# Two halves of one PSUM tile become two tiles in the first MLP, and double tiles in the second

## The chip, the core and the metric

The kernel runs on one core of one Trainium2 chip. The metric is the device time of one execution in microseconds. Before the change it is 1389.45 us, the median of three runs (1388.26 to 1395.5).

## The reference

Three stages run one after the other. Attention reads float32 inputs, the weights are float64, and the result is float32, 4608 rows and 512 columns:

```python
# attention in chunks of 64 tokens, 8 batches, 8 heads, 576 tokens, head size 64
scores = scale * np.matmul(q_c, k_c.transpose(0, 1, 2, 4, 3))
scores = scores - np.max(scores, axis=-1, keepdims=True)
attn = np.exp(scores)
attn = attn / (np.sum(attn, axis=-1, keepdims=True) + 1e-09)
out = np.matmul(attn, v_c)
# first MLP, 512 -> 2048 -> 512
h = x @ w_in
g = np.maximum(h, 0.0) + np.log1p(np.exp(-np.abs(h)))
x = g @ w_out
# second MLP, 512 -> 768 -> 512
h = np.maximum(np.maximum(x @ w1, x @ w2), x @ w3)
return (h @ w_out).astype(np.float32)
```

## The kernel before

**Splitting and blocks.** The kernel keeps about float32 precision by cutting each operand into a high and a low part and running three matmuls for each product: high with high, high with low, low with high (`PASS`, line 26). Tokens go in 9 blocks of 512 (`TB`). A matmul writes 128 rows by 512 float32 columns, which is one PSUM bank.

**Order of the work.** No engine decides at run time. Every piece of work is an `Op` with an engine, an estimated cost, a due time and the buffers (`Buf`) that it reads, writes or takes. `Plan.order` (line 106) runs a small list scheduler over them: it starts the ready operation that is due first on each engine, gives it a free place of the kind that its `Buf` names (`places`, line 214), and returns all operations in order of their planned start. They are then issued in that order (line 1599). The framework below looks at the tiles that each instruction touches and adds the semaphore waits. So the order on each engine is fixed, and an instruction that must wait holds up everything behind it on its engine. Operations of TensorE's long products are chained in one line (`in_line("h", ...)`), so that they keep the order of the program.

**First MLP, blocks 0 to 2.** `mlp1` (line 782) computes for each of 16 columns blocks `j` of the hidden layer 12 matmuls into `ph` (line 791), a softplus on ACT from `ph` into a `tmp` (line 801), the cut of that into `g`, and 12 matmuls into the accumulators `acc` (line 811). Meanwhile the float64 weights are turned into float32 parts on DVE (`conv`, `cut_up`; a sum of two parts goes through `ph` by two small matmuls, lines 398 and 399), and the attention of later tiles goes through `aps`.

**First MLP, blocks 3 to 8.** Pairs of blocks are computed with seven products instead of eight (`UnitA`, line 1067; Strassen's method). Each unit has one `ph` (`u.Y`), into which products 1, 6, 7 and 4 go one after the other, copied out in between, and uses a shared pair of banks `XZ` (tile `one`): product 2 goes to half `X`, products 5 and 3 to half `Z`, and DVE adds each to what was kept (lines 1084, 1100, 1104, 1110). Two units overlap, an old and a new one. The attention that is left runs in the same two halves (`square_of`, line 580; lines 535 to 555), and `mlp1_out` (line 1150) does the second product of the MLP into `acc` (line 1190).

**Second MLP.** `Triple` (line 1255) takes three blocks at a time and computes their hidden layers with 15 products of sums instead of 18, each 12 matmuls into a pair of banks (line 1328), which are read as one wide operand by ACT or DVE. Four pairs are used in turn (`Bank`, line 1228): `ph`, `one` and the two `acc`. The last product (line 1426) accumulates into the same four pairs.

**The tiles of the change.** `ph` is one tile of two banks, `pairh` (line 213), and the two places of the kind `ph` are its halves (line 242). In the second MLP the same tile is used whole: `halves = [Buf("ph") ...]` (line 1530). `aps` is a tile of its own pool (line 204); when the Strassen products begin, `one_by_one` (line 1207) closes that pool and puts one tile of two banks, `one`, in its place, of which `X` and `Z` are the halves:

```python
pairh = psum.tile([P, 2, TB], F32, name="ph")
"ph": [pairh[:, n] for n in range(2)],
one_of.append(single.tile([P, 2, TB], F32, name="one"))
return [one_of[0][:, n] for n in range(2)]
```

Of the kernel before, what the change touches and what calls it, by code (L numbers as in the profile page):

```python
# [10 lines left out]
F32 = mybir.dt.float32  # L11
# [6 lines left out]
PSUM = bass.MemoryType.PSUM  # L18
DRAM = bass.MemoryType.DRAM

P = 128
# [162 lines left out]
def tile_kernel(ctx: ExitStack, tc: tile.TileContext, q, k, v, w_in, w_out, w1, w2, w3, wo2, out):  # L184
# [10 lines left out]
    TB = 512  # L195
# [4 lines left out]

    pool = ctx.enter_context(tc.tile_pool(name="sb", bufs=1))
    psum = ctx.enter_context(tc.tile_pool(name="ps", bufs=1, space=PSUM))
    banks = ExitStack()
    pair_of_banks = banks.enter_context(tc.tile_pool(name="pa", bufs=1, space=PSUM))
    dram = ctx.enter_context(tc.tile_pool(name="dr", bufs=1, space=DRAM))

    def mem(kind, n, shape, dt, where=pool):
        return [where.tile(shape, dt, name=f"{kind}{i}") for i in range(n)]
# [1 line left out]
    ident = pool.tile([P, P], F32, name="ident")  # L210
    small = {"mx": mem("mx", 4, [P, H], F32), "rq": mem("rq", 1, [P, TB], F32)}

    pairh = psum.tile([P, 2, TB], F32, name="ph")
    places = {

        "w": list(range(32)),
# [22 lines left out]
        "rv": mem("rv", 1, [P, TB], F32),  # L239
        "p": mem("p", 1, [P, TB], F32),  # L240
        "pd": [dram.tile([P, TB], F32, name=f"pd{i}") for i in range(2)],
        "ph": [pairh[:, n] for n in range(2)],
        "aps": mem("aps", 1, [P, 2, TB], F32, pair_of_banks),
        "acc": mem("acc", 2, [P, 2, TB], F32, psum),
        **small,
# [693 lines left out]
    def pe2(cost, fn, **kw):  # L939
        o = in_line("h", op({"P": cost}, fn, due=clock[0], **kw))  # L940
        clock[0] += cost
        return o
# [124 lines left out]
    class UnitA:  # L1067
# [8 lines left out]
        def product(u, p, dst, first, **kw):  # L1076
            at, col, name = SEVEN[p]
            ws, x = u.ws[at], x2["a", u.q, name]
            col += HT * (u.n % 2) if at == 3 else 0

            def fn(e):
                for kk in range(2):
                    for wi, xi in PASS:
                        nc.tensor.matmul(  # L1084
                            dst(),
                            ws.t[:, wi, col + kk * P:col + (kk + 1) * P],
                            x[kk].t[:, xi],
                            start=(first and kk == 0 and wi == 0 and xi == 0),
                            stop=(kk == 1 and wi == 1),
                            skip_group_check=not first,  # L1090
                        )

            return pe2(1.36, fn, r=[ws, *x], hold=u.ring[at] + held["a", u.q, name], **kw)
# [108 lines left out]

    second = {}

    one_of = []

    def one_by_one(_):

        banks.close()
        single = ctx.enter_context(tc.tile_pool(name="pb", bufs=1, space=PSUM))  # L1210
        one_of.append(single.tile([P, 2, TB], F32, name="one"))
        return [one_of[0][:, n] for n in range(2)]

    XZ = Buf("aps", fresh=one_by_one)

# [39 lines left out]
    class Triple:  # L1255
# [44 lines left out]
                lambda: wide(XL.t), lambda: wide(R[z].t), lambda: wide(XH.t).bitcast(F32), ALU.subtract, [R[z], XH], [XL], n=1.77  # L1300
            )

        def product(u, s, d):
            if s not in u.x:
                u.split(s)
            XH, XL, token = u.x[s]
            if u.q == 0 and d in DIRECT:
                ws, ring = direct[s, d]
            else:
                ws, ring = slot("w", "x"), Buf("ringb")  # L1310
                o = op(
                    {"G": 1.0},
                    lambda e: nc.gpsimd.dma_start(out=ws.t.bitcast(F32), in_=w2c[s][d]),  # L1313
                    w=[ws],
                    alloc=[ring, ws],
                    after=[store["c", s, d]],
                    lat=2.0,
                    move=2.2,
                )
                in_line("ringb", o)  # L1320
            bank = u.spare if s in (0, 12) else u.main[d]
            first = s in (0, 1, 12)

            def fn(e):
                for f in range(2):
                    for kk in range(2):
                        for wi, xi in PASS:
                            nc.tensor.matmul(  # L1328
                                bank.view()[:, f],
                                ws.t[:, wi, f * HT + kk * P:f * HT + (kk + 1) * P],  # L1330
                                (XH, XL)[xi].t[:, kk],
                                start=(first and kk == 0 and wi == 0 and xi == 0),
                                stop=(kk == 1 and wi == 1),
                                skip_group_check=not first,
                            )

            o = pe2(2.72, fn, r=[ws, XH, XL], w=bank.bufs, alloc=bank.new(), hold=[ring, token])
            u.read(s, d, bank)
            return o

# [119 lines left out]
    def strassen():  # L1460

        outs, earlies = [], 0
        tile_at = HP * NP + 2 * HP + 2

        def out(n=1):
            for out_of, *which in outs[:n]:
                out_of(*which)
            del outs[:n]

        def group():  # L1470
            nonlocal tile_at
            if tile_at <= NTILE + 1:
                attention(tile_at, [first_loads[11]], True)
            tile_at += 1

        splita(0)
        pairs = (NB - NP) // 2
        for q in range(pairs):
            A, B = NP + 2 * q, NP + 2 * q + 1
            old = None  # L1480
            for n, m in enumerate(ORDER[q]):
                clock[0] = T0 + STEP * NJ * A + 17.7 * n
                new = UnitA(q, m)
                begin = new.p1()
                for _ in range(EARLIES[q][n]):
                    early(earlies, clock[0] + STEP * EARLY, [begin])
                    earlies += 1
                if q == pairs - 1:
                    mark[n] = begin
                out()  # L1490
                if old:
                    old.p5()
                    old.p4()
                    outs.append((mlp1_out, A, 2 * old.n + 1))
                new.p6()
                if old:
                    old.p3()
                else:
                    out()
                new.p2()  # L1500
                if not old:
                    out()
                new.p7()
                if n in GROUPS:
                    group()
                out()
                outs.append((mlp1_out, A, 2 * m))
                old = new
            clock[0] = T0 + STEP * NJ * A + 17.7 * (NJ // 2)
            mark["load", q] = begin  # L1510
            mark["late", q] = old.p4()
            outs.append((mlp1_out, A, 2 * m + 1))
            out()
            old.p5()
            out()
            old.p3()
            todo = [(mlp1_out, B, 2 * m + f) for m in ORDER[q] for f in range(2)]
            outs.extend((*todo[i], (h,)) for h in range(2) for i in range(2))
            outs.extend(todo[2:])
            for j in range(NJ - 2):  # L1520
                out()
                if j in LATE_GROUPS:
                    group()
                if j == SPLIT and q + 1 < pairs:
                    splita(q + 1)
        mark[5] = mark[6]
        clock[0] = T1
        for d, at in enumerate((mark["late", 1], mark[4], mark["late", 2])):
            weights3(d, [at])
        halves = [Buf("ph") for _ in range(2)]  # L1530
        accs = [Buf("acc") for _ in range(2)]
        banks = [Bank(halves, lambda: pairh), Bank([XZ], lambda: one_of[0])]
        banks += [Bank([z], lambda z=z: z.t) for z in accs]
        D = range(NJ2 // 2)
        gate = [mark[5]]
        for q in range(NB // 3):
            u = Triple(q, banks, gate)
            u.g = {}
            todo = [(s, d) for d in D for s in (0, 1)] + [(s, d) for s in range(2, 12) for d in D]
            todo += [(s, d) for d in D for s in (12, 13)] + [(14, d) for d in D]  # L1540
            if q == 0:
                todo[:6] = [(0, 0), None, None, (1, 0), None, None, (0, 1), (0, 2), (2, 0), (1, 1), (1, 2)]
                todo = [p for n, p in enumerate(todo) if p != (2, 0) or n < 11]
            for p in todo:
                if p is None:
                    out()
                    continue
                begin = u.product(*p)
                if p == (13, 0):
                    gate = [begin]  # L1550
            for c in range(3):
                for d in D if (q, c) != (NB // 3 - 1, 2) else D[:-1]:
                    u.out(c, d)
            banks = [u.main[1], u.main[2], u.spare, u.main[0]]
        for h in range(2):
            u.out(2, D[-1], range(2 * h, 2 * h + 2))
# [5 lines left out]
    for n, f in enumerate((1.0, -1.0)):  # L1562
# [3 lines left out]
            w=[(eye, n)],  # L1566
# [66 lines left out]
```

## Time and profile before

| | before |
|---|---|
| median of 3 runs (lowest to highest) | 1389.45 us (1388.26 to 1395.5) |
| profiled execution, its own time | 1391.89 us |
| its span, first to last instruction | 1390.1 us |
| mean granted TensorE clock | 0.992 |
| PE (matmuls) busy | 1349.2 us, 97% |
| PEld (weight loads) busy | 1104.5 us, 79% |
| DVE busy | 940.0 us, 68% |
| ACT busy | 486.8 us, 35% |
| POOL busy | 303.1 us, 22% |

PE is TensorE's matmuls, PEld its weight loads, DVE VectorE, ACT ScalarE, POOL GpSimd, SP the engine that issues most DMAs. The profile names an instruction by the line of the kernel that made it (L791), often a helper's: L276 and L278 are copies, L283 is every two-operand operation of DVE. In the timeline a row is one instruction or several of the same kind that follow each other; its first number is when it began, the second how long it took, and in brackets stands how long its engine had stood idle before it and what ended that. `ph` and `one` name a whole tile there, without the half.

### The profile page before, as it was taken

The page shows a single profiled execution, that of the slowest core. Times are in us where ns is not written, and L with a number is a line of the kernel's source. Part 1 is how long each engine was busy: PE and PEld are TensorE (multiplying, and loading weights), DVE is VectorE, ACT ScalarE, POOL GpSimd, SP SyncE. Part 2 cuts the span into 40 slices and gives each one's busy share as a digit, 9 for nine tenths or more (in the row PEclk, how much of TensorE's full clock was granted, in tenths as well). Part 3 has the DMA queues.
Part 4 walks back from the last instruction along what each step waited for, and adds up shares of the span by engine and source line. Part 5 has one row for each costly group of instructions (what it writes and reads, how often), then busy time and mean ns, then how long its engine had stood idle before and what let it go on. Part 6 is the DMA issues. An engine that isn't in the chain of part 4 may idle for free.

```text
span 1390.1 us, 22779 instructions
## 1 busy us (share of the span) xinstructions
PE 1349.2 (97%) x8664; PEld 1104.5 (79%) x8664; DVE 940.0 (68%) x1510; ACT 486.8 (35%) x790; POOL 303.1 (22%) x532
## 2 busy tenths in 40 slices
PE   5899999999999999999999999999999999999998
PEld 3677877788788788887888878788888888888887
DVE  8899976698576846637856686459824497244951
ACT  4444323354433524344434453433113221132211
POOL 2001545542142303312122112112101111011100
PEclk9999999999999999999999999999999999999999
DMA  9545657675688977857979899556644466444401
GB/s 275 163 142 141 155 162 216 189 256 175 201 238 277 258 201 210 276 172 273 314 261 341 277 359 371 197 182 227 226 168 137 151 218 221 152 152 136 151 15 76
DMA packets 221772, 288.84 MB, mean 208 GB/s; under 512 B 122096, under 2 KB 147120, under 8 KB 221664
## 3 DMA queue, kind: packets, MB, share of 16 engines
q0 software_dynamic: 49728, 163.53, 34.7%
q1 hardware_dynamic: 171120, 123.08, 29.2%
q8 instruction: 68, 1.11, 0.3%
q10 hardware_dynamic: 816, 0.79, 0.2%
q14 instruction: 40, 0.33, 0.1%
HBM read 200.28 MB, written 87.03 MB: 207 GB/s over the span
## 4 chain that ended last, share of the span: by engine, by line
PE 82%; DVE 9%; DMA 4%; issue 2%; SPq 1%; ACT 1%; POOL 1%; DVEq 0%; ACTq 0%; POOLq 0%
PE acc L1190 17%; PE acc L1328 14%; PE ph L1084 8%; PE one L1328 8%; PE one L1084 6%; PE ph L791 5%; PE acc L811 5%; PE ph L1328 5%; PE acc L1426 5%; PE one L1426 3%; PE ph L1426 3%; DVE s L283 1%; DVE tmp L283 1%; PE one L583 1%; DVE tmp L346 1%
## 5 line engine op out<-in xcount | busy, mean ns | idle before, releaser
L1190 PE MATMUL acc<-g,s 128*128 128x512 f32 x1152 | 278.0, 394 | 3.8 <-DVE g L283 2.2
L1190 PEld LDWEIGHTS acc<-g,s 128*128 128x128 f32 x1152 | 216.2, 189 | 52.3 <-DVE g L283 4.7
L283 DVE TENSOR_TENSOR s<-s,s 128x512 fp32r<-128x512 f32 (+3 forms) x252 | 222.8, 906 | 41.6 <-ACT s L276 33.0
L276 ACT CAST s<-s 128x1024 fp32r<-128x1024 f32 (+1 forms) x140 | 115.3, 839 | 244.8 <-DVE s L283 86.9
L1328 PE MATMUL acc<-s,s 128*128 128x512 f32 x852 | 200.1, 389 | 0.0
L1328 PEld LDWEIGHTS acc<-s,s 128*128 128x128 f32 x852 | 159.9, 188 | 33.2
L283 DVE TENSOR_TENSOR g<-tmp,g 128x512 fp32r<-128x512 f32 x132 | 90.1, 684 | 94.3 <-ACT g L276 92.1
L791 PE MATMUL ph<-s,s 128*128 128x512 f32 x576 | 143.5, 400 | 4.7 <-ACT tmp L801 4.7
L1313 POOL DMA_DIRECT2D s<-w2c x120 | 63.9, 533 | 365.8 <-PE acc L1328 105.5
L1084 PE MATMUL ph<-s,s 128*128 128x512 f32 x576 | 142.9, 389 | 0.0
L811 PE MATMUL acc<-g,s 128*128 128x512 f32 x576 | 139.8, 392 | 0.1
L791 PEld LDWEIGHTS ph<-s,s 128*128 128x128 f32 x576 | 109.6, 192 | 30.2 <-ACT tmp L801 6.5
L1084 PEld LDWEIGHTS ph<-s,s 128*128 128x128 f32 x576 | 108.2, 188 | 22.6
L811 PEld LDWEIGHTS acc<-g,s 128*128 128x128 f32 x576 | 107.3, 188 | 23.3 <-ACT tmp L276 0.5
L1328 PE MATMUL one<-s,s 128*128 128x512 f32 x468 | 112.4, 389 | 0.0
L1084 PE MATMUL one<-s,s 128*128 128x512 f32 x432 | 106.2, 389 | 0.0
L1328 PEld LDWEIGHTS one<-s,s 128*128 128x128 f32 x468 | 87.8, 188 | 18.2
L276 ACT CAST g<-tmp 128x512 fp32r<-128x512 f32 x128 | 79.4, 621 | 48.5 <-PE acc L1190 34.4
L1084 PEld LDWEIGHTS one<-s,s 128*128 128x128 f32 x432 | 81.1, 188 | 16.8
L463 POOL DMA_DIRECT2D rv<-in_v_dram x102 | 62.0, 612 | 142.2 <-PE one L583 95.3
L1110 ACT ACTIVATE tmp<-tmp 128x512 f32<-128x512 f32 x72 | 45.0, 632 | 126.9 <-DVE tmp L283 126.8
L283 DVE TENSOR_TENSOR tmp<-one,tmp 128x512 f32<-128x512 f32 x72 | 48.1, 685 | 52.1 <-PE one L1084 48.6
(138 smaller groups left out, 1648.2 us busy)
## 6 DMA issues: line engine op xcount, KB each, us to landing
s<-w2c POOLq DMA_DIRECT2D x120, 512.0 KB, 4.3
s<-wac POOLq DMA_DIRECT2D x66, 512.0 KB, 5.9
w2c<-s POOLq DMA_DIRECT2D x45, 512.0 KB, 5.5
wac<-s POOLq DMA_DIRECT2D x24, 512.0 KB, 5.2
gd<-tmp SPq DMA_DIRECT2D x48, 256.0 KB, 4.4
x2d<-tmp SPq DMA_DIRECT2D x36, 256.0 KB, 4.3
s<-in_moe_w_dram POOLq DMA_DIRECT2D x18, 512.0 KB, 5.1
tmp<-gd SPq DMA_DIRECT2D x36, 256.0 KB, 5.0
```

The lines of the kernel that those rows point to most:

```text
L276: nc.scalar.copy(dst(), src())
L283: return op({"D": 0.69 * n}, lambda e: nc.vector.tensor_tensor(dst(), a(), b(), f), r=r, w=w, **kw)
L346: lambda e: nc.vector.scalar_tensor_tensor(ai(), hw(), -0x40000000, ai(), ALU.bitwise_and, ALU.bitwise_or),
L463: dma(out=dst().rearrange("p (c e d) -> p c e d", e=2, d=D)[half * CH:(half + 1) * CH, lo:lo + mine, h, :], in_=v[b, t % HP * 2 + h].rearr ...
L791: nc.tensor.matmul(ph.t, w[:, wi, kk * P:(kk + 1) * P], x[kk].t[:, xi], start=(kk == 0 and wi == 0 and xi == 0), stop=(kk == KD - 1 and wi ...
L811: nc.tensor.matmul(acc[m // 2].t[:, m % 2], w[:, wi, m * P:(m + 1) * P], g.t[:, gi, :], start=(first and wi == 0 and gi == 0), stop=(last ...
L1084: nc.tensor.matmul(dst(), ws.t[:, wi, col + kk * P:col + (kk + 1) * P], x[kk].t[:, xi], start=(first and kk == 0 and wi == 0 and xi == 0), ...
L1110: in_line("y", op({"A": 0.62}, lambda e: nc.scalar.activation(c.t, src(), AF.Softplus), r=[z], w=[c], alloc=[] if z is c else [c]))
L1190: nc.tensor.matmul(acc[half].t[:, m % 2], w.t[:, wi, m * P:(m + 1) * P], g.t[:, gi, :], start=(first and wi == 0 and gi == 0), stop=(last ...
L1313: lambda e: nc.gpsimd.dma_start(out=ws.t.bitcast(F32), in_=w2c[s][d]),
L1328: nc.tensor.matmul(bank.view()[:, f], ws.t[:, wi, f * HT + kk * P:f * HT + (kk + 1) * P], (XH, XL)[xi].t[:, kk], start=(first and kk == 0 ...
L1426: nc.tensor.matmul(banks[t // 2].view()[:, t % 2], (GH, GL)[gi].t[:, f, t * P:(t + 1) * P], wo2_of[j].t[:, wi], start=(j == 0 and wi == 0 ...
```

## The change

The change makes the two halves of `ph` two tiles of one bank, in a pool of their own, and the two halves `X` and `Z` of `one` two tiles as well. When the second MLP begins, `four_banks` closes both pools and puts two tiles of two banks, `both`, in their place. For that the first product of the second MLP takes three places together: the two of `ph` and the one of `aps`. The second MLP's first two pairs of banks are then these double tiles. The accumulators, all loops and all costs and due times stay.

```diff
--- before.py
+++ after.py
@@ -200,6 +200,8 @@
 
     pool = ctx.enter_context(tc.tile_pool(name="sb", bufs=1))
     psum = ctx.enter_context(tc.tile_pool(name="ps", bufs=1, space=PSUM))
+    halves = ExitStack()
+    pair_of_halves = halves.enter_context(tc.tile_pool(name="pp", bufs=1, space=PSUM))
     banks = ExitStack()
     pair_of_banks = banks.enter_context(tc.tile_pool(name="pa", bufs=1, space=PSUM))
     dram = ctx.enter_context(tc.tile_pool(name="dr", bufs=1, space=DRAM))
@@ -210,7 +212,6 @@
     ident = pool.tile([P, P], F32, name="ident")
     small = {"mx": mem("mx", 4, [P, H], F32), "rq": mem("rq", 1, [P, TB], F32)}
 
-    pairh = psum.tile([P, 2, TB], F32, name="ph")
     places = {
 
         "w": list(range(32)),
@@ -239,7 +240,7 @@
         "rv": mem("rv", 1, [P, TB], F32),
         "p": mem("p", 1, [P, TB], F32),
         "pd": [dram.tile([P, TB], F32, name=f"pd{i}") for i in range(2)],
-        "ph": [pairh[:, n] for n in range(2)],
+        "ph": mem("ph", 2, [P, TB], F32, pair_of_halves),
         "aps": mem("aps", 1, [P, 2, TB], F32, pair_of_banks),
         "acc": mem("acc", 2, [P, 2, TB], F32, psum),
         **small,
@@ -1202,14 +1203,16 @@
 
     second = {}
 
-    one_of = []
-
     def one_by_one(_):
-
         banks.close()
-        single = ctx.enter_context(tc.tile_pool(name="pb", bufs=1, space=PSUM))
-        one_of.append(single.tile([P, 2, TB], F32, name="one"))
-        return [one_of[0][:, n] for n in range(2)]
+        single = banks.enter_context(tc.tile_pool(name="pb", bufs=1, space=PSUM))
+        return mem("one", 2, [P, TB], F32, single)
+
+    def four_banks(_):
+        banks.close()
+        halves.close()
+        again = ctx.enter_context(tc.tile_pool(name="pq", bufs=1, space=PSUM))
+        return mem("both", 2, [P, 2, TB], F32, again)
 
     XZ = Buf("aps", fresh=one_by_one)
 
@@ -1300,7 +1303,7 @@
                 lambda: wide(XL.t), lambda: wide(R[z].t), lambda: wide(XH.t).bitcast(F32), ALU.subtract, [R[z], XH], [XL], n=1.77
             )
 
-        def product(u, s, d):
+        def product(u, s, d, alloc=()):
             if s not in u.x:
                 u.split(s)
             XH, XL, token = u.x[s]
@@ -1334,7 +1337,7 @@
                                 skip_group_check=not first,
                             )
 
-            o = pe2(2.72, fn, r=[ws, XH, XL], w=bank.bufs, alloc=bank.new(), hold=[ring, token])
+            o = pe2(2.72, fn, r=[ws, XH, XL], w=bank.bufs, alloc=[*alloc, *bank.new()] if not alloc else alloc, hold=[ring, token])
             u.read(s, d, bank)
             return o
 
@@ -1527,9 +1530,9 @@
         clock[0] = T1
         for d, at in enumerate((mark["late", 1], mark[4], mark["late", 2])):
             weights3(d, [at])
-        halves = [Buf("ph") for _ in range(2)]
+        both = [Buf("ph"), Buf("ph"), Buf("aps", fresh=four_banks)]
         accs = [Buf("acc") for _ in range(2)]
-        banks = [Bank(halves, lambda: pairh), Bank([XZ], lambda: one_of[0])]
+        banks = [Bank(both[:1], lambda: both[2].t[0]), Bank(both[1:], lambda: both[2].t[1])]
         banks += [Bank([z], lambda z=z: z.t) for z in accs]
         D = range(NJ2 // 2)
         gate = [mark[5]]
@@ -1545,7 +1548,7 @@
                 if p is None:
                     out()
                     continue
-                begin = u.product(*p)
+                begin = u.product(*p, alloc=both if both[0].first is None else [])
                 if p == (13, 0):
                     gate = [begin]
             for c in range(3):
```

## Rows read from the trace of the kernel before

**Rows 1.** The page: the span, and part 1, busy us (share) xinstructions.

```profile
span 1390.1 us, 22779 instructions
...
PE 1349.2 (97%) x8664; PEld 1104.5 (79%) x8664; DVE 940.0 (68%) x1510; ACT 486.8 (35%) x790; POOL 303.1 (22%) x532
```

**Rows 2.** The list of waits: engine line <- released by: us, times, longest us.

```profile
PE ph L791 <- ACT tmp L801: 4.7, 5, 2.2
...
PE ph L398 <- ACT tmp L801: 2.8, 1, 2.8
PE one L583 <- DMA s<-gd: 2.7, 1, 2.7
...
PE acc L1190 <- DVE g L283: 2.2, 4, 0.8
...
ACT tmp L1110 <- PE ph L1084: 27.8, 21, 1.4
```

**Rows 3.** Timeline, 79 to 87: start us, us, engine, line, operation, xcount, [idle before <-releaser].

```profile
79.87 5.60 PE L791 MATMUL ph<-s,s 128*128 128x512 f32 x24
...
85.51 0.60 ACT L801 ACTIVATE tmp<-ph 128x512 f32<-128x512 f32 x1 [2.71 <-PE ph L791]
...
86.16 3.01 PE L791 MATMUL ph<-s,s 128*128 128x512 f32 x12 [0.69 <-ACT tmp L801]
```

**Rows 4.** Timeline, 344 to 347: `ph`, then `one`, then the copy of `ph`.

```profile
344.12 1.52 PE L1084 MATMUL ph<-s,s 128*128 128x512 f32 x6
...
345.48 1.52 PE L1084 MATMUL one<-s,s 128*128 128x512 f32 x6
345.68 0.59 ACT L276 COPY tmp<-ph 128x512 f32<-128x512 f32 x1 [3.49 <-PE ph L1084]
```

**Rows 5.** Timeline, 254 to 263, around the longest wait of L791.

```profile
254.90 0.58 ACT L801 ACTIVATE tmp<-ph 128x512 f32<-128x512 f32 x1
...
255.53 7.36 PE L791 MATMUL ph<-s,s 128*128 128x512 f32 x24 [2.18 <-ACT tmp L801]
```

**Rows 6.** Stretches: length; PE, PEld, DVE, ACT, POOL busy (count); granted clock; DMA share, GB/s.

```profile
113.00:180.00 67.00, 66.89 (x410) 54.30 (x409) 67.00 (x139) 25.71 (x44) 21.93 (x35) 1.00 0.52 133
257.00:259.00 2.00, 2.00 (x7) 1.51 (x6) 2.00 (x4) 0.00 (x0) 0.89 (x3) 0.50 0.29 71
644.00:646.00 2.00, 2.00 (x6) 1.52 (x6) 2.00 (x5) 0.33 (x2) 0.64 (x1) 0.50 1.03 405
```

**Rows 7.** Timeline, 36 to 63, the start of the first MLP.

```profile
36.56 0.63 PE L399 MATMUL ph<-s,s 128*128 128x512 f32 x1
...
41.88 0.69 DVE L283 TENSOR_TENSOR s<-ph,tmp 128x512 fp32r<-128x512 f32 x1 [3.52 <-PE ph L791]
...
49.80 0.69 PE L498 MATMUL aps<-ident,s 64*64 64x64 f32 x32 [1.31 <-DMA s<-in_v_dram]
...
50.32 0.65 PE L498 MATMUL acc<-s,s 64*64 64x64 f32 x32
...
51.71 0.68 DVE L558 TENSOR_REDUCE mx<-acc 128x8 f32<-128x512 f32 x1
...
61.83 0.69 PE L498 MATMUL acc<-ident,tmp 64*64 64x64 f32 x32 [1.22 <-ACT s L276]
```

**Rows 8.** Timeline, 458 to 461, in the Strassen products.

```profile
458.53 0.60 ACT L1110 ACTIVATE tmp<-ph 128x512 f32<-128x512 f32 x1 [1.36 <-PE ph L1084]
...
459.81 0.69 DVE L283 TENSOR_TENSOR g<-tmp,g 128x512 fp32r<-128x512 f32 x1 [0.81 <-ACT g L276]
```

**Rows 9.** Timeline, 642 to 649: the longest wait of that stage and what follows.

```profile
642.38 1.23 PE L583 MATMUL one<-s,rv 64*64 64x64 f32 x32 [2.69 <-DMA s<-gd]
...
643.54 5.41 PE L1190 MATMUL acc<-g,s 128*128 128x512 f32 x12
```

**Rows 10.** Timeline, 825 to 862: last reading of `one`, first product of the second MLP.

```profile
825.03 0.68 DVE L283 TENSOR_TENSOR tmp<-one,tmp 128x512 f32<-128x512 f32 x1
...
859.08 2.88 PE L1328 MATMUL ph<-s,s 128*128 128x512 f32 x12
```

## The prediction

> **What bounds the kernel now.** I read the page's busy shares first: TensorE's matmuls (PE) cover 1349.2 of 1390.1 us [rows 1]. A change that adds and removes no matmul can only win the 41 us in which PE stands still, and matmuls that run at the lower clock. The list of waits says who PE waits for [rows 2]. Two of its lines bear on the first MLP's pair of banks `ph`: five times a product L791 waits for the softplus L801, 4.7 us together, and once the small product L398 waits for it, 2.8 us.
>
> The timeline shows why. From 79.87 two products follow each other, 24 matmuls in 5.60 us, one per half of `ph` [rows 3]. The first half is complete near 82.7, yet its softplus starts at 85.51, after 2.71 us of waiting for PE: it waited for the other half's product. The third product needs the first half back and starts at 86.16, 0.69 us late. Where two tiles are written one after the other it is different: the copy of `ph` starts at 345.68, when the six matmuls on `ph` end (344.12 + 1.52), while six on `one` run from 345.48 [rows 4]. So a reader waits for all earlier writes to its tile, not for PE's queue as a whole. The semaphores follow tiles, and half against half costs a wait that no data need.
>
> That is where a rule and this trace part. The Trainium skill, PSUM — Partial Sum Buffer, section on bank collisions, asks only for a guard by bank (and quadrant). If these waits already went by bank, halves in two banks would not order each other, the change would free nothing, and the sum below would be 0. The softplus at 85.51 speaks against that [rows 3].
>
> **The change, part by part.** *No work is added or removed.* Matmuls, copies, softplus and DMAs stay. The planner's costs and due times are untouched, and a half is one place of `ph` before and after, so I expect the same order on every engine. SP's and POOL's queues are passed by nothing. What goes are semaphore waits between the halves of `ph` and between `X` and `Z` of `one`; the second MLP again works on two-bank tiles and keeps its waits.
>
> *The five waits of L791.* When a third product needs half A, and the softplus of half B is what ends its wait, the wait is false; in the first case the softplus itself was held up falsely. I credit all five: 4.70 us. Bounds: 0 if the true reader of the half is equally late, 4.70 at most. The largest is the clearest: at 255.53 PE had stood 2.18 us, until a softplus queued on ACT behind an attention step had read one half at 254.90 [rows 5]; the halves go by turns, and the product needed the other. A group after a break also fills anew: 12 matmuls took 3.01 us at 86.16, against 2.80 for half of the 24 [rows 3]. Between 0 and 0.21 us each I take 0.1, so 0.5 us.
>
> *The clock behind the longest wait.* The 24 matmuls at 255.53 took 7.36 us instead of 5.60 [rows 3, 5]; the granted clock was 0.50 from 257 to 259 [rows 6], the lower of the two levels (1.2 GHz). PE had just stood still for 2.18 us. Without the break I expect 2.4 GHz: 7.36 - 5.60 - 0.1 = 1.66 us. Bounds: 0 and 1.76.
>
> *The start.* A sum in `ph` ended at 37.19 (36.56 + 0.63), but DVE could read it only at 41.88, 3.52 us later than it was free to, because L791 was filling the other half [rows 7]; PE later lost the 2.8 us at L398 [rows 2]. Both go, but I count little: at 49.80 PE waits for a load, whose issue on SP does not depend on this. PE arrives earlier and waits longer there. DVE, ahead by 3.5 us, meets the scores of that tile, complete at 50.97 (50.32 + 0.65), which it reads at 51.71: 0.74 us of lead is left. At 61.83 PE had waited 1.22 us for that stream. I take 0.65 us, a little under DVE's lead; bounds 0 and 2.8.
>
> *The Strassen products of the first MLP.* PE waits for neither `ph` nor `one` there, but ACT does, falsely: at 458.53 a softplus had idled 1.36 us for the other half, and DVE 0.81 us behind it [rows 8]; there are 21 waits of L1110 for `ph`, the longest 1.4 us [rows 2]. DVE's cover is gone where PE waits for its `g`: four times, 2.2 us [rows 2]. DVE's 0.81 us is as much as the longest of these (0.8), but other work of DVE stands ahead of the later ones. Between 0 and 2.2 I take half, 1.1 us. The largest wait there, 2.69 us at 642.38 [rows 9], names a DMA, and I leave it standing; should it shrink enough to keep the clock (0.50 from 644 to 646 [rows 6]), 12 matmuls would not take 5.41 us but 2.80 to 3.01 [rows 3, 9], some 2.5 us more.
>
> *The move to the second MLP.* Its first product now takes four banks at once: it must follow the last reader of `one`, which ends at 825.71, and starts at 859.08 [rows 10]. Some 33 us cover this; cost 0. If that cover were gone, each us past it would be one of PE's. PE carries on behind it, so what is won before reaches the end.
>
> *Sum:* 4.70 + 0.5 + 1.66 + 0.65 + 1.1 = 8.61 us. The profiled execution took 1391.89 us (1.79 around its span) and would take 1383.3. It is 2.44 above the median of the three runs, 1389.45; the same gain from the median gives **1380.8 us**. About 0.5% (7 us) is what a measurement here can tell from no change.
>
> **The rivals.** *Given back later.* PE arrives earlier, and the next true dependency holds it. DVE is busy for all 67 us from 113 to 180 [rows 6], so weights may come no sooner; against it, PE itself is full there and DVE loses false waits as well. Then only the 255 us wait with its clock and some of the rest stay: 2.18 + 1.66 = 3.8 us, 1385.6 us.
>
> *More than the sum.* The 642 us stretch keeps its clock, and the upper ends of the start and of `g` hold: 8.61 + 2.5 + 2.1 + 1.1 = 14.3 us, 1375.1 us.
>
> *It does not do what it says.* If nothing was ordered half against half and the softplus was late for another reason, the time stays 1389.5. The two readers, one released at once and one not, are hard to read that way [rows 3, 4]. The bank rule of the Trainium skill, applied to these waits, would end here.
>
> *Slower: the clock.* If the moved work makes PE stand still anew at two places as at 642.38, each costs its 2.69 us of idling and 2.5 us of slow matmuls. Two cost 10.4 us, and against the 8.61 won the time is 1391.2. It decides once new breaks cost more than 8.61 us together. For it: the wait at 642.38 shows that such breaks exist [rows 9]. Against it: the change adds no work that could make one, it only moves work earlier.
>
> **How the numbers follow.** Forecast (6 to 11 us won) 0.50, given back 0.26, more 0.13, nothing 0.07, slower 0.04. The likeliest gives 1380.8. The range goes from the "more" case, 1374.5, to 1388.0, which takes in the give-back and leaves out the last two cases. Faster by over 0.5% means under 1382.5: four fifths of the forecast and all of "more", 0.53. Slower than 1396.4 needs the clock case at its worst, 0.02; the rest, 0.45, is no change. The forecast's own range is 1378.5 to 1383.5.
>
> **What would show it right or wrong.** In the changed profile L801 should start when its own product ends, with L791 already on the next; the line "L791 waits for L801" should vanish, and the softplus L1110 should lose its 1.36 us waits. The clock should stay 1.0 near 255. At 49.80 PE's wait for the load should grow by about what the 2.8 us wait gave. The first product of the second MLP should show no wait. I am wrong if L801 still starts only after a second product, if new waits on DVE or DMA sum to the old ones, or if the clock falls at new places.

## The result, and the profile after

The changed kernel takes 1377.88 us, the median of five runs (1376.32 to 1381.74); the kernel before took 1390.26 us in the five runs beside it. The ratio is 0.9911, with a 95% interval of 0.9885 to 0.9936: faster by 0.9%. The forecast was 1380.8. The profiled execution took 1377.88 us, too.

From the page of the kernel after come the span, the busy time of each engine and the shares of the chain of work that ended last.

```profile
span 1376.1 us, 22799 instructions
...
PE 1344.3 (98%) x8664; PEld 1103.5 (80%) x8664; DVE 940.8 (68%) x1510; ACT 492.5 (36%) x790; POOL 303.4 (22%) x532
...
PE 90%; DVE 5%; DMA 2%; issue 1%; POOL 0%; ACT 0%; SPq 0%; POOLq 0%; DVEq 0%; ACTq 0%
```

The work is the same [rows 1]: as many instructions on each engine, DVE, ACT and POOL about as busy. (The 20 more in the total are semaphore instructions, which carry the waits.) The order on each of the five engines is that of before, instruction for instruction; only the waits differ. PE is 4.9 us less busy (1.4 of it in L792 and 1.5 in L584), and of the 14.0 us by which the span is shorter the other 9.1 are idling that went. The chain that ended last runs over PE for 90% of the span (82% before). Lines after the change have moved: L791 is L792, L801 is L802, L398 is L399, L583 is L584, L1190 is L1191.

PE's waits in the kernel after (us in all, times, longest us):

```profile
PE acc L499 <- DMA s<-in_q_dram: 5.3, 1, 5.3
...
PE acc L1191 <- ACT tmp L277: 3.3, 1, 3.3
...
PE one L584 <- DVE tmp L284: 1.8, 1, 1.8
...
PE both L1331 <- ACT s L277: 1.1, 1, 1.1
PE acc L1191 <- DVE g L284: 1.0, 2, 0.7
PE aps L499 <- issue: 0.8, 1, 0.8
```

"L792 waits for L802" and "L399 waits for L802" are gone, which were 4.7 and 2.8 us [rows 2]. The 2.7 us wait of L583, put down to a DMA, has become one of L584 of 1.8 us, put down to DVE; it is the same instruction. New is 3.3 us of L1191 for an ACT copy.

The timeline of the kernel after from 77 to 87, the place of [rows 3]:

```profile
77.78 8.32 PE L792 MATMUL ph<-s,s 128*128 128x512 f32 x36
...
80.70 0.60 ACT L802 ACTIVATE tmp<-ph 128x512 f32<-128x512 f32 x1
...
83.42 0.60 ACT L802 ACTIVATE tmp<-ph 128x512 f32<-128x512 f32 x1 [1.47 <-PE ph L792]
...
86.14 0.60 ACT L802 ACTIVATE tmp<-ph 128x512 f32<-128x512 f32 x1 [0.94 <-PE ph L792]
```

Three products run as one row of 36 matmuls. The softplus starts 2.92, 5.64 and 8.36 us into it, each as its own 12 matmuls end, while PE fills the other half. That is what the prediction said the softplus would do.

Timeline of the kernel after, the start of the first MLP, answering [rows 7]:

```profile
38.22 0.69 DVE L284 TENSOR_TENSOR s<-ph,tmp 128x512 fp32r<-128x512 f32 x1
...
41.40 0.59 ACT L802 ACTIVATE tmp<-ph 128x512 f32<-128x512 f32 x1
...
42.24 0.50 PE L399 MATMUL ph<-s,s 128*128 128x512 f32 x1
...
45.78 0.64 PE L499 MATMUL aps<-ident,s 64*64 64x64 f32 x29 [0.79 <-issue]
...
58.16 0.69 PE L499 MATMUL acc<-ident,tmp 64*64 64x64 f32 x32 [1.22 <-ACT s L277]
```

DVE reads the sum at 38.22 without waiting, where it had waited 3.52 us. The product of L399 starts at 42.24 instead of 45.70. The instruction that had waited 1.31 us for a load at 49.80 is at 45.78, with 0.79 us put down to issue.

The place of the longest wait of L791 [rows 5], and the granted clock in three stretches (columns as in [rows 6]):

```profile
247.01 5.38 PE L792 MATMUL ph<-s,s 128*128 128x512 f32 x23
...
248.67 0.58 ACT L802 ACTIVATE tmp<-ph 128x512 f32<-128x512 f32 x1
```

```profile
60.00:62.00 2.00, 2.00 (x6) 1.57 (x7) 2.00 (x5) 1.31 (x2) 0.00 (x0) 0.58 0.56 101
257.00:259.00 2.00, 2.00 (x11) 1.62 (x10) 1.66 (x3) 0.52 (x2) 0.73 (x3) 1.00 0.48 93
812.00:816.00 4.00, 3.67 (x9) 2.89 (x10) 0.37 (x2) 0.98 (x3) 0.00 (x0) 0.50 1.05 414
```

PE no longer stops in front of 247.01, and the clock there stays at 2.4 GHz: 23 matmuls in 5.38 us, where 24 had taken 7.36. The clock fell in two stretches where it had not in the kernel before: 60 to 64 us (0.58) and 812 to 816 us (0.50).

Timeline of the kernel after, at the places of [rows 9] and [rows 10]:

```profile
628.16 0.79 PE L584 MATMUL one<-s,rv 64*64 64x64 f32 x32 [1.80 <-DVE tmp L284]
...
628.88 3.01 PE L1191 MATMUL acc<-g,s 128*128 128x512 f32 x12
...
806.64 0.68 DVE L284 TENSOR_TENSOR tmp<-one,tmp 128x512 f32<-128x512 f32 x1
...
845.09 2.88 PE L1331 MATMUL both<-s,s 128*128 128x512 f32 x12
```

The stop in front of L584 is 1.80 us, and the 12 matmuls behind it took 3.01 us, at full clock, not 5.41. The double tile `both` is first written at 845.09, 38 us after the last reading of `one`, and PE does not wait for it.

The new wait lies in front of the last part of the first MLP. These are pieces of the chain that leads there (start, us, what), in the kernel after:

```profile
805.58 6.09 DMA gd<-tmp
...
811.70 0.59 ACT tmp L277
...
812.34 2.93 PE acc L1191 x6
```

A copy out of an accumulator needs a `tmp` whose store was issued at 805.58 and landed 6.09 us later. PE then starts, after 3.30 us of waiting, at the low clock (0.50). The Trainium skill, Perfetto Trace Analysis, section "DMA Instruction — HWDGE (DVE, Sync)", says that the semaphore ending a transfer comes only when the write is complete, which can take surprisingly long for HBM. The 6.09 us here are long, against a median of 4.5 for the stores of this kind, but the trace does not show which part of them is that.

### The profile page after: what moved, and what is told of

It reads as the page before. It is cut to its first block, busy times and chain, and to the rows that moved or that the text cites. A ratio compares the mean times of both kernels' runs of the same rounds, so it can differ in the third digit from the quotient of the medians.

```text
span 1376.1 us, 22799 instructions
## 1 busy us (share of the span) xinstructions
PE 1344.3 (98%) x8664; PEld 1103.5 (80%) x8664; DVE 940.8 (68%) x1510; ACT 492.5 (36%) x790; POOL 303.4 (22%) x532
## 4 chain that ended last, share of the span: by engine, by line
PE 90%; DVE 5%; DMA 2%; issue 1%; POOL 0%; ACT 0%; SPq 0%; POOLq 0%; DVEq 0%; ACTq 0%
PE acc L1191 18%; PE acc L1331 14%; PE both L1331 13%; PE acc L812 9%; PE ph L792 9%; PE ph L1085 9%; PE one L1085 6%; PE both L1429 6%; PE acc L1429 5%; PE aps L499 1%; PE one L584 1%; DVE s L284 1%; DVE tmp L284 1%; DMA tmp<-in_q_dram 1%; DVE tmp L347 0%
## 5 line engine op out<-in xcount | busy, mean ns | idle before, releaser
L1191 PE MATMUL acc<-g,s 128*128 128x512 f32 x1152 | 277.7, 394 | 4.5 <-ACT tmp L277 3.3
L1191 PEld LDWEIGHTS acc<-g,s 128*128 128x128 f32 x1152 | 216.6, 189 | 52.4 <-ACT tmp L277 3.7
L1331 PE MATMUL both<-s,s 128*128 128x512 f32 x768 | 181.7, 389 | 1.1 <-ACT s L277 1.1
L1331 PEld LDWEIGHTS both<-s,s 128*128 128x128 f32 x768 | 144.1, 188 | 31.4 <-ACT s L277 1.5
L792 PE MATMUL ph<-s,s 128*128 128x512 f32 x576 | 142.2, 398 | 0.0
L792 PEld LDWEIGHTS ph<-s,s 128*128 128x128 f32 x576 | 109.5, 192 | 23.6
L1085 PE MATMUL one<-s,s 128*128 128x512 f32 x432 | 106.2, 389 | 0.0
L1085 PEld LDWEIGHTS one<-s,s 128*128 128x128 f32 x432 | 81.1, 188 | 16.8
```

Of the source, the lines that this page charges most:

```text
L792: nc.tensor.matmul(ph.t, w[:, wi, kk * P:(kk + 1) * P], x[kk].t[:, xi], start=(kk == 0 and wi == 0 and xi == 0), stop=(kk == KD - 1 and wi ...
L1085: nc.tensor.matmul(dst(), ws.t[:, wi, col + kk * P:col + (kk + 1) * P], x[kk].t[:, xi], start=(first and kk == 0 and wi == 0 and xi == 0), ...
L1191: nc.tensor.matmul(acc[half].t[:, m % 2], w.t[:, wi, m * P:(m + 1) * P], g.t[:, gi, :], start=(first and wi == 0 and gi == 0), stop=(last ...
L1331: nc.tensor.matmul(bank.view()[:, f], ws.t[:, wi, f * HT + kk * P:f * HT + (kk + 1) * P], (XH, XL)[xi].t[:, kk], start=(first and kk == 0 ...
```

## The experiments

The first four kernels ran on one chip, the other three on another, each with runs of the kernel before beside them. The first three part the change: only `ph` split, only `one` split, neither, all with the new pools and `both`.

**Only `ph` split** (against the changed kernel):

```diff
-        return mem("one", 2, [P, TB], F32, single)
+        one = single.tile([P, 2, TB], F32, name="one")
+        return [one[:, n] for n in range(2)]
```

> The changed kernel, but X and Z of `one` are again halves of one tile; only `ph` is two tiles. Theory (false waits between halves, most of them in ph): the changed kernel took 12.4 us less than the one before (medians 1377.9 and 1390.3). By the ledger of TensorE's starts in the two traces, 10.1 us of the lead are there before the first product of the Strassen stage, where only ph matters, so about 1380 us, 1378 to 1382; the softplus of ph starts when its own product ends, and what is lost against the change lies after 340 us. Rival (the two tiles of `one` bring it, since DVE and ACT share them with the attention): near 1390. Rival (placement of the banks): the placement is that of the change, so 1378.

Measured: 1380.46 us (6 runs), ratio 0.9938 (0.9918 to 0.9957). **Only `one` split:**

```diff
-        "ph": mem("ph", 2, [P, TB], F32, pair_of_halves),
+    pairh = pair_of_halves.tile([P, 2, TB], F32, name="ph")
+        "ph": [pairh[:, n] for n in range(2)],
```

> The other half of the change alone: X and Z are two tiles, ph is one tile of two halves. Theory: the five waits of L791 and the wait at the start return, the stretch up to 340 us is that of the kernel before, and the gain is what DVE and ACT win in the Strassen stage: 1387 to 1390 us. With the first run the two parts should add up to about the whole, 12.4 us, unless the lower clock after a long wait comes or goes. Rival (the gain comes from `one`): near 1378.

Measured: 1385.57 us (12 runs), ratio 0.9968 (0.9955 to 0.9981). That is under the expected 1387 to 1390, but the kernel before took 1388.05 us beside it, not 1390.3. **Neither split**, with both edits:

> The pools, the bank numbers, the new double tiles and the three places taken together as in the change, but both pairs are again one tile each with two halves. Theory: nothing but the waits matters, so the time is that of the kernel before, 1390.3 us within 0.3%, with the five waits of L791 back in the trace. Rival (bank placement or the new double tiles of the second MLP bring the gain): near 1378 us. The wait at the start that the profile gave to a load (1.31 us at 49.80 before) is back if it belongs to the loads, and absent if it hung on the order of events behind L398.

Measured: 1389.01 us (12 runs), ratio 1.0003 (0.9989 to 1.0017). So it is the splitting that counts, not the pools, the new places or the double tiles in the second MLP. The two parts add up: 0.9938 times 0.9968 is 0.9906, and the whole change has 0.9911. By the ratios `ph` brings about two thirds and `one` a third; by the medians, 7.6 and 2.5 us, it is three quarters and one.

PE's waits with only `one` split, where L793 is the product into `ph`, L803 its softplus and L400 the small product; the last line is from ACT's waits, L1112 being the softplus of the Strassen products:

```profile
PE ph L400 <- ACT tmp L803: 2.8, 1, 2.8
...
PE ph L793 <- ACT tmp L803: 2.1, 4, 0.7
```

```profile
ACT tmp L1112 <- PE ph L1086: 27.9, 21, 1.4
```

All the false waits on `ph` are back: 2.8 us, four times of L793, and the 21 waits of ACT for `ph` [rows 2]. Still this kernel is faster than before. (Its profiled execution, 1380.85 us, is 4.7 us under its median, so its row below flatters it.) Where it gains shows when the traces are cut at five PE instructions, the same in every kernel (us between them; they began at 49.80, 260.43, 638.16, 825.90 and 894.94 in the trace before; the last column is the rest up to the last matmul's start):

| kernel | to 49.80 | to 260.43 | to 638.16 | to 825.90 | to 894.94 | rest |
|---|---|---|---|---|---|---|
| before | 49.80 | 210.63 | 377.73 | 187.74 | 69.03 | 490.28 |
| neither split | 49.65 | 207.09 | 377.89 | 186.95 | 71.35 | 490.28 |
| only `ph` | 45.13 | 204.17 | 377.77 | 186.47 | 69.30 | 490.28 |
| only `one` | 48.30 | 205.95 | 374.77 | 184.15 | 70.76 | 490.28 |
| the change | 45.78 | 204.40 | 374.65 | 182.68 | 73.43 | 490.28 |
| the change again | 45.52 | 203.92 | 375.81 | 183.75 | 74.25 | 490.28 |
| the change, freer `tmp` | 45.78 | 202.94 | 374.56 | 183.27 | 67.97 | 490.60 |
| the same again | 45.78 | 206.73 | 374.43 | 182.78 | 67.75 | 490.55 |
| before, freer `tmp` | 49.41 | 209.84 | 377.77 | 185.23 | 67.13 | 490.56 |

Up to some 800 us the three kernels with a freer `tmp`, of which more below, have the same order as their partners without it, so there they count as further executions of those. From 260 to 638 all four kernels with `one` joined agree within 0.16 us, whether `ph` is split or not; the five with it split take 1.9 to 3.5 us less. What `one` held up stands in the timeline: first with only `ph` split, then, of the same place, with only `one` split.

```profile
349.25 2.88 PE L1085 MATMUL one<-s,s 128*128 128x512 f32 x12
...
351.97 1.52 PE L1085 MATMUL ph<-s,s 128*128 128x512 f32 x6
...
352.17 0.69 DVE L284 TENSOR_TENSOR tmp<-one,tmp 128x512 f32<-128x512 f32 x1 [2.04 <-PE one L1085]
...
353.40 0.65 DVE L284 TENSOR_TENSOR tmp<-one,tmp 128x512 f32<-128x512 f32 x1
...
354.11 0.73 PE L584 MATMUL one<-s,rv 64*64 64x64 f32 x29 [0.62 <-DVE tmp L284]
```

```profile
354.19 2.88 PE L1086 MATMUL one<-s,s 128*128 128x512 f32 x12
...
356.35 0.68 DVE L285 TENSOR_TENSOR tmp<-one,tmp 128x512 f32<-128x512 f32 x1
...
356.91 1.52 PE L1086 MATMUL ph<-s,s 128*128 128x512 f32 x6
...
357.57 0.65 DVE L285 TENSOR_TENSOR tmp<-one,tmp 128x512 f32<-128x512 f32 x1
...
358.36 0.71 PE L585 MATMUL one<-s,rv 64*64 64x64 f32 x32
```

The 12 matmuls are two products, six for each half, and DVE reads one half after the other. With `one` joined it can read the first half only when the second is written too (352.17, 2.92 us after the 12 began), and it had idled 2.04 us for that. Its second reading ends at 354.05, and the attention's matmuls of L584 start 0.06 us later. With the halves split the first reading starts 2.16 us after the 12 began, without idling, and the second ends 4.03 us after them instead of 4.80. L585 then starts 1.45 us after the product in front of it instead of 2.14, and no wait is listed. So the false wait is DVE's, as it was ACT's for `ph`, and PE pays for it one step later. In the four kernels with `one` joined 26 of DVE's 72 such readings start over 1.2 us after their half was written, in the five with it split one or two. Most of what PE loses by it is too short to be listed: the lead of only-`one` over only-`ph` in this stage grows at eleven groups of L584, by 0.78 us here, 0.23 at one and 0.19 at each of nine, 2.7 of the 3.0 in all. In the kernel with `one` joined each of the eleven starts 0.05 or 0.06 us after DVE's reading.

**A freer `tmp`.** The late wait was tested by letting the copies out of the accumulators take one of five kinds of buffer (rq, rk, rv, p or `tmp`), not `tmp` alone, in one of the blocks. The planner answers with another order on DVE, ACT and POOL from some 800 us on, and two operations go from ACT to DVE, so from there it is not the buffers alone that differ:

```diff
-            o = Buf("tmp")
+            o = Buf(*(LATE if b == NB - 2 else ("tmp",)))
```

> The changed kernel, and the accumulators of the last pair's first block are copied out into the four buffers that attention no longer needs (rq, rk, rv, p) instead of tmp. In the changed kernel TensorE stands still for 3.30 us at 812.34, behind a copy that waits 2.21 us for a tmp whose store has not landed, and runs at the lower clock for some us after it (the lead over the kernel before falls from 18.4 to 14.2 us there). Theory: the break goes or falls below 1.5 us, the clock stays, and the time falls by 3 to 5.5 us against the change, to 1372.5 to 1375. Rival (something else is late next, the gd loads or the DMA queues that are full there): no gain, 1377 to 1379, and a break of the same length a little later.

Measured: 1374.76 us (6 runs), ratio 0.9901 (0.9878 to 0.9924). The wait is gone, but 0.9901 against 0.9911 lies within the intervals. So it was run again on another chip, beside the change and beside the kernel before with this one edit.

> The changed kernel once more, as the partner of the next two on one chip, and for a second profile. Theory: 0.989 to 0.993 of the kernel before. The waits that come from the order of work (none of L791 for a softplus, one of L584 near 628, one of L1191 near 812) are there again; where the clock falls behind them may differ, since the four profiles with and without the change already differ in that: behind the wait near 640 the clock fell in three of five, and behind the one of L791 near 255 in one of three. Rival (the clock's falls belong to the program): the same falls at the same places, near 61 and near 812.

> The kernel before, with the accumulators of the last pair's first block copied into the buffers that attention no longer needs. It tells whether what that edit wins depends on the change. In the profile of before, L1190 waits 1.53 us at 828.96 for that copy, in the profile with both tiles joined 2.3 us with a fall of the clock. Theory: the wait goes in either kernel, 1.5 to 4 us, 1384 to 1387 where the kernel before takes 1388. Rival (only the change made that wait matter, as it brought the store nearer): no difference.

> The changed kernel with the free buffers again, beside the change itself on one chip. Theory: 3 to 5 us below the change in this call, about 1373 to 1375, with no wait of L1191 for a copy near 810. Rival (the gap of the first call, 0.9901 against 0.9911, is all there is): 1 us or less.

Measured there, with six, 12 and six runs: the change 1379.49 us (0.9929, 0.9905 to 0.9953), the kernel before with a freer `tmp` 1385.97 (0.9986, 0.9973 to 0.9998), both together 1374.78 (0.9900, 0.9882 to 0.9919). PE's waits in the change run again, then in the kernel before with a freer `tmp`:

```profile
PE acc L1191 <- ACT tmp L277: 4.3, 1, 4.3
...
PE acc L1191 <- DVE g L284: 2.9, 4, 1.1
```

```profile
PE ph L398 <- ACT tmp L801: 2.8, 1, 2.8
...
PE ph L791 <- ACT tmp L801: 2.4, 4, 0.8
PE acc L1190 <- DVE g L283: 2.3, 4, 0.8
```

In the second the wait for ACT's copy does not appear, as in both kernels of the change with the edit. Without the change the edit is worth 0.14%, with it 4.7 us, or 0.34% by the medians; these two gains are not told apart by so few runs. The wait itself is: in the three kernels with `one` joined and the old `tmp` it was 1.5 (before), 1.8 and 2.3 us; in the three with `one` split it is 3.3, 3.3 and 4.3. That PE reaches the place sooner while the store takes what it took is the likely reason. In the table this is the column "to 894.94": 73.4 and 74.3 us with the change, 67 to 68 us in all three kernels with the edit. Both together is the fastest version here, 1% below the kernel before.

## Why the prediction was right, and where its steps were off

**The mechanism held.** The semaphores follow tiles. At 77.78 each softplus starts at its own product's end (elsewhere some still start later, behind ACT's other work or other waits), the five waits are gone, so is the line of the Strassen softplus that waited for `ph`, the order is that of before, and the move to the second MLP costs nothing. The rival that nothing was ordered half against half falls with the third experiment: the same banks, the same pools, and only the tiles joined gave 1.0003. The bank rule of the Trainium skill (PSUM — Partial Sum Buffer, section "PSUM bank collisions raise a hardware error") says what must be guarded; these waits were wider than that. Another of its pages, Perfetto Trace Analysis, section "Matmuls", advises turning through different banks so that reading one group overlaps the next. The kernel before did so, and at 79.87 [rows 3] it gained no overlap, because both banks were one tile.

One sign of being wrong that the prediction named did come: the clock fell at new places. The fall at 60 us was not there in the second profile of the change, the one at 812 us was.

**The total was 12.4 us between the medians, against 8.61,** and 8.8 us on the second chip (1388.3 to 1379.49). That the sum came this near is in part luck, as its terms show:

*The five waits with their refill and the 255 us clock,* 4.70 + 0.5 + 1.66. In the two profiles first compared they were nearly right: the lead of PE grew from 2.39 us at 65.5 to 10.14 at 259.4, by 7.75. But a good part belonged to one execution. Over the same stretch the four kernels with `ph` joined took 189.3 to 193.9 us and the five with it split 185.7 to 189.5, a difference of 4.9 us in the mean, against 6.86. In the three other kernels with `ph` joined, L791 waits 2.1, 2.1 and 2.4 us in four times, 0.8 at the longest, and the 24 matmuls at that place take 5.60 to 5.74 us. With neither split the wait at that place is 0.32 us:

```profile
253.44 5.73 PE L793 MATMUL ph<-s,s 128*128 128x512 f32 x24 [0.32 <-ACT tmp L803]
```

So these 2.18 + 1.66 us, the clearest stop in the trace, are not what the kernel pays there each time. One profile could not tell that.

*The start* was priced at 0.65, and here the step failed that said "at 49.80 PE waits for a load, whose issue on SP does not depend on this. PE arrives earlier and waits longer there". The table's first column gives 45.1 to 45.8 us in all five kernels with `ph` split, against 48.3 to 49.8 in the four with it joined: 2.5 to 4.7 us. About 1 us of it is given back in the attention that follows; at 65.5, 2.7 us are left in the mean, four times the price and just under my upper bound of 2.8. The promised growth of that wait did not come. The row named a DMA as the last releaser, but the load was not a wall. These are SP's issues of the loads of which it named one, before and after:

```profile
44.07 14.61 SPq L463 DMA_DIRECT2D s<-in_v_dram  x18
```

```profile
45.87 14.30 SPq L464 DMA_DIRECT2D s<-in_v_dram  x18
```

In the kernel after, the instruction at 45.78 had started before the first of the 18 was issued, so it needs none of them. In the kernel before with a freer `tmp`, where PE's order is the same, these instructions ran without a stop.

```profile
48.56 1.53 PE L498 MATMUL aps<-ident,s 64*64 64x64 f32 x64
```

Why it stood 1.31 us there in the first profile stays open; with neither split it stood 1.09, put down to issue. In the change's first profile 1.27 us of the start went back by 65.5, in matmuls at the low clock (60 to 64 us); in its second run the clock there was 1.00.

*The Strassen products* were priced at 1.1 us, and the step named the wrong tile. It took the softplus that waits for `ph`, DVE behind it, and PE's waits for `g`. With only `ph` split the waits of ACT for `ph` are gone from the list, and PE is not a tenth of a microsecond faster from 260 to 638, with the same 2.2 us of waits for `g`:

```profile
PE acc L1191 <- DVE g L284: 2.2, 4, 0.8
```

The gain came from `one`, by way of DVE's readings and L584, in delays mostly too short for the list of waits: 1.9 to 3.5 us up to 638, and in the mean of the rows 3.3 more up to 826, clock included. I had written that PE waits for neither tile there.

*The wait at 642.38,* which I left standing because its row names a DMA, gave more: 0.9 us of idling and 2.8 of clock between the two profiles (PE's lead went from 13.31 to 17.05). The DMA was the wrong reading here too. In the trace before, DVE's last reading of `one` ends 0.06 us in front of it:

```profile
641.65 0.67 DVE L283 TENSOR_TENSOR tmp<-one,tmp 128x512 f32<-128x512 f32 x1
```

In all nine traces that instruction starts within 0.06 us of the end of this reading, so what hastens DVE shortens the wait: 2.69 us in the four kernels with `one` joined, 1.80 to 2.46 in the five with it split. The part of the clock is less sure, since one of the four kept its clock behind the 2.69 us (last section). That is the "more than the sum" rival, come in part.

*Given back later* came in part as well: the wait at 812.34, 1.77 us above that of before, and its 12 matmuls at the low clock, 2.4 us, took the lead from 18.39 to 14.23. Start, `one` and 642 were under-priced, the five waits over-priced and this rival left out of the sum, so the errors partly cancelled, and the range held.

## What to carry to other kernels

Where buffers are used in turn, look in the timeline whether a reader starts when its own part is written or when the neighbour's is; if the latter, make them tiles of their own, with no change of order or place. Look at every engine that reads them, and compare the start times of the same instructions, since many small delays stand in no list of waits. Don't price a stop by the one execution that shows it at its largest, nor take a DMA named as releaser for a wall: look what else ended just before. After such a gain look for the next wait down the line: here a buffer still being stored, which cost 1.5 us of waiting before the change and 3.3 or 4.3 with it.

## What was not expected of the hardware

The clock's fall behind a stop comes and goes between executions of nearly the same work. In front of L583 near 640 four kernels stop for 2.69 us: the kernel before, only `ph`, neither, and before with a freer `tmp`. The clock fell behind it in the first three and not in the fourth. Here are the stop and the two microseconds behind it (columns as in [rows 6]), with neither split and in the kernel before with a freer `tmp`:

```profile
638.85 1.23 PE L585 MATMUL one<-s,rv 64*64 64x64 f32 x32 [2.69 <-DVE tmp L285]
```

```profile
640.00:642.00 2.00, 2.00 (x8) 1.61 (x6) 2.00 (x5) 0.75 (x3) 0.00 (x0) 0.51 0.99 392
```

```profile
641.23 0.79 PE L583 MATMUL one<-s,rv 64*64 64x64 f32 x32 [2.69 <-DMA s<-gd]
```

```profile
642.00:644.00 2.00, 2.00 (x11) 1.66 (x10) 2.00 (x5) 1.04 (x3) 0.64 (x1) 1.00 1.05 411
```

The stop is the same to 0.01 us, and the clock 0.51 in the one and 1.00 in the other.

Behind the late wait it fell with the change both times and with neither split (0.57 from 826 to 830), but not with only `one` split, where PE had waited 3.3 us. Each fall that is priced above cost 1.3 to 2.8 us, so by estimate two or three of them would be a good part of the 4 to 10 us by which runs of one kernel differ. What decides it, these runs don't show.
